# Attention emitted by a table of times per quad of heads, with four score banks and the value product among the transposes' banks

## The chip, the cores and the metric

The kernel runs on one core of a Trainium2 chip. Its engines are PE (matmul), DVE (VectorE), ACT (ScalarE), POOL (GpSimd) and SP (which here only issues DMAs). The metric is device time in microseconds (us), lower is better.

## What is computed

Three stages in a row: windowed attention with a few global tokens, a mixture of experts with one expert per token, and a dense two-layer net.

```
s_g  = scale * q_g @ k_all^T ; out_g = softmax(s_g) @ v_all      # 32 global queries, 544 keys
s_ll = scale * q_l @ k_l^T, masked to |i - j| <= 32              # 512 local queries
s_l  = concat(scale * q_l @ k_g^T, s_ll) ; out_l = softmax(s_l) @ concat(v_g, v_l)
x    = concat(out_g, out_l), 2176 rows (4 batches x 544) of 512 (8 heads x 64)
e    = argmax(x @ w_gate) ; x = gate * relu(x @ w1[e]) @ w2[e]   # 8 experts, one per token
h    = x @ w_in ; g = 0, (h+1)^2/4 or h by pieces ; out = g @ w_out
```

There are 32 heads in all (4 batches of 8). All data is float32; the matmuls of the second and third stage are split into three products of rounded parts, those of the attention are plain float32.

## The kernel before

The change lies in the attention, the first 124 us. The other stages follow it in the program.

**Tiles.** Heads are worked in pairs (`c`, 16 of them) and quads (`q`, 8 of them, two pairs each). The steps, with the letters used below, are:

- G, `s_glob(q)`: scores of a quad's global queries, 12 matmuls into a score bank `sp` and a corner of the bank `gxb`; needs `qg` and the keys of both pairs. GM (`g_max`), GE (`g_exp`), GN (`g_norm`): their maximum on DVE, exponentials on ACT, reciprocal on DVE. TG (`t_glob`): six transposes into two `ps_o` banks, copied out by ACT. PG (`pv_glob`): product with the values of both pairs.
- S, `s_pair(c)`: scores of a pair's two heads, 64 small matmuls and two mask matmuls into two `sp` banks. M (`s_max(n)`): maximum of one head on DVE. E (`s_exp(n)`): four exponentials on ACT. T (`t_head(n)`): four transposes on PE into a `ps_o` bank, copied to `pto` by DVE.
- P, `pv(c)`: product of a pair with its values, 64 matmuls into a bank `xo`, scaled by DVE into `xr`. X (`x_turn`): four transposes of `xr` into a `ps_x` bank, copied by ACT into `xT`. XS (`x_store`): the store of two pairs.
- L and LT (`logits`, `logits_t`), then R (`route`): the gate of one batch, some nine small DVE operations. `early` follows it: a few small matmuls (`ranks`), six to eight DVE operations (`place`) and four POOL operations (`low_hot`). They are put into the list `fill`, of which F (`s_rest`) emits up to eight at a time. `zlist` is a last short chain of matmuls on what `low_hot` wrote. Z runs what stands in `tasks`.
- V and K: loads of values (three DMAs for a pair), keys and queries. V also has POOL spread a pair's values (`spread_v`).

**Banks.** Eight in PSUM: `gxb`, three of tag "s" for scores (S and G), one of tag "x" for `xo`, three of tag "to" for transposes and logits.

**Order.** The program order is the order on each engine: each of PE, DVE, ACT and SP works its instructions strictly as emitted. Before, a loop over 40 steps (`units`, one head or one quad's global part each) emits them: a step first turns the head of two steps ago, then emits its scores, its maxima, the products that are due and its exponentials. The steps of the quads 0, 1 and 7 are moved by hand. After the loop the last two heads, the last two products and the remaining turns are written out. SP's loads are paced: each waits until those more than 1.5 MB ahead of it have landed (`dma`).

Of the kernel before, what the change touches and what calls it, by code (L numbers as in the profile page):

```python
# [8 lines left out]
F32 = mybir.dt.float32  # L9
# [15 lines left out]
B, H, SL, SG, D = 4, 8, 512, 32, 64  # L25
# [5 lines left out]
S = SL + SG  # L31
N = B * S
NT = N // 128
E, F = 8, 1024
# [89 lines left out]
def emit(tc, d, out):  # L124
# [55 lines left out]
    wz = ap.tile([128, 2], F32, name="wz")  # L180
    nc.vector.memset(wz, 0.0)
    nc.scalar.activation(wz[:, 1:2], wz[:, 0:1], AF.Exp)
    wps = ps.tile([128, 512], F32, tag="s", name="sp", bufs=3)
    for _ in range(9):
        nc.tensor.matmul(wps, lhsT=warm[:, 0:128], rhs=warm, start=True, stop=True)
    qp = {}
# [57 lines left out]
    def s_pair(c):  # L244
        k, q = ks[c], qp[c]
        for z in range(2):
            home, n = ("x", 1) if c == 1 and z else ("s", 3)
            sps[2 * c + z] = ps.tile([128, 4, BW], F32, tag=home, name="sp", bufs=n)
        for j in range(NG):
            i, a = divmod(j, 4)  # L250
            for z in range(2):
                r = slice(64 * z, 64 * z + 64)
                nc.tensor.matmul(sps[2 * c + z][a * WIN:(a + 1) * WIN, i, :], lhsT=q[r, j * WIN:(j + 1) * WIN],  # L253
                                 rhs=k_at(k, r, j), start=(i == 0), stop=False)
        for z in range(2):
            nc.tensor.matmul(sps[2 * c + z][:, :, 0:MW], lhsT=mask[:, 0:128], rhs=mask[:, 128:].rearrange("p (i w) -> p i w", i=4), start=False, stop=True)
# [24 lines left out]
        pexp[n] = p  # L281

    def s_glob(q):
        sp = ps.tile([128, 512], F32, tag="s", name="sp", bufs=3)
        for part in range(3):
            for j in range(4):
                c, z = 2 * q + j // 2, 64 * (j % 2)
                k = ks[c][z:z + 64].rearrange("p (n w) -> p n w", w=WIN)
                p = slice(j * SG, (j + 1) * SG)
                o, r = ((sp[p, 0:320], ks[c][z:z + 64, 0:320]),  # L290
                        (sp[p, 320:480], k[:, 15:24:2, :]), (gxb[p, 0:64], k[:, 10:13:2, :]))[part]
                nc.tensor.matmul(o, lhsT=qg[z:z + 64, c, :], rhs=r, start=True, stop=True)
        gsp[q] = sp
# [75 lines left out]
    def pv(c):  # L369
        b, g = divmod(c, 4)  # L370
        p, v = pt.pop(c), vt[c]
        if g == 0:
            xr[b] = ap.tile([128, 4, DM], F32, tag="xr", name="xr", bufs=2)
            xT[b] = ap.tile([128, 4, SL], F32, tag="xT", name="xT", bufs=2)
        xo = ps.tile([128, 4, 2, D], F32, tag="s" if c == 15 else "x", name="xo", bufs=3 if c == 15 else 1)
        for i in range(4):
            for z in range(2):
                for a in range(4):
                    j = 4 * i + a
                    nc.tensor.matmul(xo[a * WIN:(a + 1) * WIN, i, z, :], lhsT=p[:, z, j * WIN:(j + 1) * WIN],  # L380
                                     rhs=v[:, v_at(j), 64 * z:64 * z + 64], start=True, stop=True)
        r = ap.tile([128, 4, 2], F32, tag="ri", name="ri", bufs=3)
        nc.vector.tensor_scalar_add(r, ss[b][:, :, 2 * g:2 * g + 2], 1e-9)
        nc.vector.reciprocal(r, r)
        nc.vector.tensor_tensor(xr[b][:, :, g * 128:(g + 1) * 128].rearrange("p i (z d) -> p i z d", z=2), xo,
                                r.unsqueeze(3).to_broadcast([128, 4, 2, D]), ALU.mult)
# [175 lines left out]
    def zsteps():  # L562
        o = ps.tile([128, 4, 128], F32, tag="to", name="ps_x", bufs=3)
        for k in range(4):
            nc.tensor.transpose(o[:, k, :], xz[:, k * 128:(k + 1) * 128], ident)
        nc.scalar.activation(xzT, o, AF.Copy)
        yield
        for g in range(2):
            o = ps.tile([128, 4, 128], F32, tag="x" if g else "s", name="zh", bufs=1 if g else 3)
            for u in range(4):  # L570
                f = slice((4 * g + u) * 128, (4 * g + u + 1) * 128)
                for k in range(4):
                    nc.tensor.matmul(o[:, u, :], lhsT=w1r[k][:, f], rhs=xzT[:, k, :], start=(k == 0), stop=(k == 3))
                    if u < 3 or k < 3:
                        yield
            nc.scalar.activation(hz[g], o, AF.Relu)
            yield
        o = ps.tile([128, 512], F32, tag="y", name="yp", bufs=2)
        for u in range(4):
            c = slice(u * 128, (u + 1) * 128)  # L580
            for f in range(8):
                nc.tensor.matmul(o[:, c], lhsT=w2r[f // 2][:, f % 2, c], rhs=hz[f // 4][:, f % 4, :], start=(f == 0), stop=(f == 7))
                if (u, f) in ((2, 7), (3, 3)):
                    yield
        yz = mp.tile([128, YW], F32, tag="y", name="y", bufs=3)
        nc.scalar.activation(yz[:, 0:DM], o, AF.Copy)
        for u in range(4):
            nc.sync.dma_start(ys[u][:, 0:128], yz[:, u * 128:(u + 1) * 128])
        put_ids(xz, zpos)
# [4 lines left out]
        for _ in range(n):  # L594
            next(zgen, None)

    units = []
    for q in range(8):
        units += [("g", q), ("h", 4 * q), ("h", 4 * q + 1), ("h", 4 * q + 2), ("h", 4 * q + 3)]
    units.remove(("g", 0))  # L600
    units.insert(3, ("g", 0))
    units.remove(("g", 1))
    units.insert(7, ("g", 1))
    units.remove(("g", 7))
    units.insert(units.index(("h", 27)), ("g", 7))
    raw = [lambda k=k: dma(w1r[k], d["w1"][0, k * 128:(k + 1) * 128, :]) for k in range(4)]
    raw += [lambda k=k: dma(w2r[k], d["w2"][0, k * 256:(k + 1) * 256, :].rearrange("(t p) f -> p t f", p=128))
            for k in range(4)]
# [5 lines left out]
    nc.sync.dma_start(ident, d["ident"])  # L614
    load_k(1)
    load_q(1)
    load_v(0)
    nc.sync.dma_start(qg, d["qg"])
    load_k(2)
    load_q(2)  # L620
    load_v(1)
# [10 lines left out]
    nc.gpsimd.tensor_copy(gid[:, :, 1:2], C("ids").unsqueeze(2))  # L632
    for c in range(3):
        spread_v(c)
    pend_n, pend_g, pend_v = [], [], []
    moved.clear()
    LT, LG = 2, 3
    nv = 3
    for s in range(len(units)):
        kind, a = units[s]  # L640
        tk, ta = units[s - LT] if s >= LT else (None, None)
        if tk == "h":
            t_head(ta)
        gq = units[s - LG] if s >= LG else (None, None)
        if gq[0] == "g":
            t_glob(gq[1])
            pend_g.append(gq[1])
        if kind == "h":
            if a % 2 == 0 and a != 2:
                s_pair(a // 2)  # L650
            if a == 1:
                s_pair(1)
        elif kind == "g":
            s_glob(a)
        while tasks:
            if tasks.pop(0)() == 1:
                break
        if kind == "h" and a % 2 == 1:
            if a // 2 + 4 < 16:
                load_k(a // 2 + 4)  # L660
            if a // 2 + 3 < 16:
                load_q(a // 2 + 3)
        if (kind, a) == ("g", 0):
            s_max(3)
        if kind == "h" and a < 31 and a != 3:
            s_max(a)
        if kind == "h" and a == 30:
            s_max(31)
        elif kind == "g":
            g_max(a)  # L670
        if (kind, a) == ("g", 0):
            s_exp(3)
        for q in pend_g:
            if gq == ("g", q):
                continue
            pv_glob(q)
        for c in pend_v:
            pv(c)
            if nv < 16:
                load_v(nv)  # L680
                nv += 1
            if 0 < c < 14:
                spread_v(c + 2)
            b, g = divmod(c, 4)
            if g % 2:
                tasks.append(lambda b=b, g=g: x_store(b, g // 2))
            tasks.append(lambda b=b, g=g: x_turn(b, g))
            if b < B - 1 and g == 3:
                then = [lambda b=b: tasks.append(lambda: early(b))]
                tasks += [lambda b=b: logits(b), lambda b=b: logits_t(b),  # L690
                          lambda b=b, then=then: fill.extend(route(b) + then)]
        for q in pend_n:
            g_norm(q)
        pend_n, pend_g, pend_v = [], [q for q in pend_g if gq == ("g", q)], []
        if tk == "h" and ta % 2 == 1:
            pend_v.append(ta // 2)
        if kind == "h" and a != 3:
            s_exp(a)
        elif kind == "g":
            g_exp(a)  # L700
            pend_n.append(a)
        if kind == "h":
            s_rest(RATE)
        for _ in range([7, 5, 3, 1].count(len(units) - s)):
            raw.pop(0)()
    assert not fill, len(fill)
    weigh(xz, 128, nc.gpsimd)
    t_head(30)
    pv(14)
    t_head(31)  # L710
    for t in tasks:
        t()
    dma(xs[B * SL:N, 0:DM], xrg)
    glob_turn()
    pv(15)
# [753 lines left out]
```

## Time and profile before

| | |
|---|---|
| median of 3 runs | 740.49 us (738.86 to 744.5) |
| profiled execution | 741.64 us, of which the profile spans 739.8 us |
| PE busy | 711.3 us (96%) |
| DVE, ACT, POOL busy | 486.1 (66%), 332.1 (45%), 150.2 us (20%) |
| mean granted TensorE clock | 0.992 |

How to read it: the first S starts at 4.80 us and the last P ends at 123.38 us; that stretch is the attention. The profiled execution lies 1.15 us above the median. Busy shares over the whole span say little about the attention, since it is one sixth of it.

### The profile page before, as it was taken

How to read it: one execution, taken by the hardware profiler on the slowest of the kernel's cores; microseconds unless marked ns; L12 is line 12 of the kernel's file. 1: busy time of each engine (PE TensorE's matmuls, PEld its weight loads, DVE VectorE, ACT ScalarE, POOL GpSimd, SP SyncE). 2: the span in 40 equal slices, each digit the busy share in tenths (PEclk: the TensorE clock that was granted, in tenths of full speed). 3: DMA queues.
4: the chain of work that ended last, by engine and by line, in shares of the span. 5: the costliest groups of instructions: out<-in, count | busy, mean ns of one | idle time of the engine just before them, and what ended most of it. 6: DMA issues, size and time to landing. Idle time of an engine off the chain costs nothing.

```text
span 739.8 us, 16419 instructions
## 1 busy us (share of the span) xinstructions
PE 711.3 (96%) x6609; PEld 637.6 (86%) x6609; DVE 486.1 (66%) x887; ACT 332.1 (45%) x762; POOL 150.2 (20%) x185
## 2 busy tenths in 40 slices
PE   6889888999999999999999999999999999999995
PEld 4666666999999999899998898999989898998984
DVE  4778885674516478875777678758775876645443
ACT  4757664453525457664564543233323332322220
POOL 3445543677641340000000000000000000011112
PEclk9999999999999999999999999999999999999998
DMA  8786666485658578763531321101110100001111
GB/s 280 237 258 202 203 194 186 134 291 196 190 166 301 199 252 305 244 208 104 122 99 58 105 68 57 58 1 58 57 58 1 58 0 1 1 30 57 43 43 71
DMA packets 52254, 96.07 MB, mean 130 GB/s; under 512 B 9817, under 2 KB 27769, under 8 KB 50128
## 3 DMA queue, kind: packets, MB, share of 16 engines
q1 hardware_dynamic: 48704, 84.75, 36.1%
q0 software_dynamic: 3472, 10.25, 4.2%
q8 instruction: 53, 0.87, 0.5%
q14 instruction: 25, 0.20, 0.1%
HBM read 80.28 MB, written 14.75 MB: 128 GB/s over the span
## 4 chain that ended last, share of the span: by engine, by line
PE 79%; issue 8%; DVE 7%; ACT 2%; DMA 2%; POOL 1%; SPq 0%; POOLq 0%; ACTq 0%; DVEq 0%
PE fh L988 7%; PE fh L986 7%; PE fh L987 7%; PE o L988 6%; PE o L987 6%; PE o L986 6%; PE hp L988 4%; PE hp L986 4%; PE hp L987 4%; PE yp L986 4%; PE yp L987 4%; PE yp L988 4%; PE ps_o L335 2%; PE sp L253 2%; DMA ks<-in_k 2%
## 5 line engine op out<-in xcount | busy, mean ns | idle before, releaser
L1318 DVE SCALAR_TENSOR_TENSOR r<-r 128x384 f32<-128x384 f32 (+1 forms) x96 | 51.4, 535 | 113.4 <-ACT r L1317 113.4
L986 PE MATMUL o<-wh,gh 128*128 128x512 f32 x272 | 106.9, 393 | 0.8 <-ACT acc L1367 0.8
L988 PE MATMUL o<-wh,gl 128*128 128x512 f32 x272 | 107.6, 396 | 0.0
L987 PE MATMUL o<-wl,gh 128*128 128x512 f32 x272 | 107.3, 394 | 0.0
L1371 POOL DMA_INDIRECT out_dram<-acc,rid x17 | 16.5, 969 | 446.4 <-DVE acc L1369 444.8
L1320 ACT ACTIVATE gh<-g 128x384 fp32r<-128x384 f32 (+1 forms) x96 | 48.8, 508 | 129.2 <-DVE g L1319 129.2
L988 PE MATMUL fh<-yh,wl 128*128 128x384 f32 (+1 forms) x320 | 104.3, 326 | 0.0
L986 PE MATMUL fh<-yh,wh 128*128 128x384 f32 (+1 forms) x320 | 104.2, 326 | 0.0
L987 PE MATMUL fh<-yl,wh 128*128 128x384 f32 (+1 forms) x320 | 104.2, 326 | 0.0
L1317 ACT ACTIVATE r<-fh,half 128x384 f32<-128x384 f32 (+1 forms) x96 | 54.0, 562 | 105.6 <-PE fh L988 105.0
L986 PEld LDWEIGHTS fh<-yh,wh 128*128 128x128 f32 x320 | 60.2, 188 | 3.5
L987 PEld LDWEIGHTS fh<-yl,wh 128*128 128x128 f32 x320 | 60.2, 188 | 3.4
L988 PEld LDWEIGHTS o<-wh,gl 128*128 128x128 f32 x272 | 51.1, 188 | 12.4 <-DVE gl L1326 0.4
L988 PEld LDWEIGHTS fh<-yh,wl 128*128 128x128 f32 x320 | 60.2, 188 | 0.0
L986 PEld LDWEIGHTS o<-wh,gh 128*128 128x128 f32 x272 | 51.1, 188 | 9.1 <-ACT acc L1367 1.2
L987 PEld LDWEIGHTS o<-wl,gh 128*128 128x128 f32 x272 | 51.1, 188 | 8.1
L280 ACT ACTIVATE p<-sp,mn 128x128 f32<-128x128 f32 x128 | 45.2, 373 | 20.0 <-DVE mn L263 10.1
L1319 DVE TENSOR_TENSOR g<-r,fh 128x384 f32<-128x384 f32 (+1 forms) x96 | 51.0, 532 | 3.3
L986 PE MATMUL yp<-hTh,w2h 128*128 128x256 f32 (+5 forms) x176 | 51.7, 294 | 0.0
L988 PE MATMUL yp<-hTh,w2l 128*128 128x256 f32 (+5 forms) x176 | 51.2, 291 | 0.0
L987 PE MATMUL yp<-hTl,w2h 128*128 128x256 f32 (+5 forms) x176 | 51.1, 290 | 0.0
L1326 DVE TENSOR_TENSOR gl<-g,gh 128x384 fp32r<-128x384 f32 (+1 forms) x96 | 50.7, 529 | 0.0
(238 smaller groups left out, 1617.3 us busy)
## 6 DMA issues: line engine op xcount, KB each, us to landing
w1r<-in_w SPq DMA_DIRECT2D x32, 512.0 KB
w2r<-in_w SPq DMA_DIRECT2D x32, 512.0 KB
wraw<-in_wf SPq DMA_DIRECT2D x16, 1024.0 KB
ks<-in_k SPq DMA_DIRECT2D x16, 400.0 KB
v<-in_v SPq DMA_DIRECT2D x16, 384.0 KB
yr<-ys SPq DMA_DIRECT2D x68, 64.0 KB
qp<-in_q SPq DMA_DIRECT2D x16, 256.0 KB
xs<-xr SPq DMA_DIRECT2D x8, 512.0 KB
```

The source lines that it names most:

```text
L253: nc.tensor.matmul(sps[2 * c + z][a * WIN:(a + 1) * WIN, i, :], lhsT=q[r, j * WIN:(j + 1) * WIN], rhs=k_at(k, r, j), start=(i == 0), stop= ...
L280: nc.scalar.activation(p[:, i, :].rearrange("p (a b w) -> p a b w", a=2, b=2), v, AF.Exp, bias=mn[:, i:i + 1], scale=scale, accum_out=ss[b ...
L335: nc.tensor.transpose(o[:, i, :], p[:, i, :], ident)
L986: nc.tensor.matmul(o, lhsT=ah, rhs=bh, start=first, stop=False)
L987: nc.tensor.matmul(o, lhsT=ah, rhs=bl, start=False, stop=False)
L988: nc.tensor.matmul(o, lhsT=al, rhs=bh, start=False, stop=last)
L1317: nc.scalar.activation(r[:, 0:w], o[:, 0:w], AF.Relu, bias=half, scale=0.5)
L1318: nc.vector.scalar_tensor_tensor(r[:, 0:w], r[:, 0:w], 1.0, r[:, 0:w], ALU.min, ALU.mult)
L1319: nc.vector.tensor_tensor(g[:, 0:w], r[:, 0:w], o[:, 0:w], ALU.max)
L1320: nc.scalar.activation(gh[:, 0:w], g[:, 0:w], AF.Copy)
L1326: nc.vector.tensor_tensor(gl[:, 0:w], g[:, 0:w], gh[:, 0:w].bitcast(F32), ALU.subtract)
L1371: w = nc.gpsimd.indirect_dma_start(out=out, out_offset=bass.IndirectOffsetOnAxis(ap=rid[:, tt:tt + 1].bitcast(U32), axis=0), in_=a, in_off ...
```

## The change

The loop over `units` is replaced by a table: each step has one or more times in units of a quad (`TIMES`), quad `q` adds `q` to them, `SHIFT` moves the global steps of quads 0 and 1, and all steps are emitted in the order of their times. The banks of tag "x" go to the scores, which have four ("s"); `xo` is put among the three of tag "to". The load of `qg` is issued before the first values. The first four expert weights (`W`) have times of their own.

```diff
-            home, n = ("x", 1) if c == 1 and z else ("s", 3)
-            sps[2 * c + z] = ps.tile([128, 4, BW], F32, tag=home, name="sp", bufs=n)
+            sps[2 * c + z] = ps.tile([128, 4, BW], F32, tag="s", name="sp", bufs=4)
...
-        xo = ps.tile([128, 4, 2, D], F32, tag="s" if c == 15 else "x", name="xo", bufs=3 if c == 15 else 1)
+        xo = ps.tile([128, 4, 2, D], F32, tag="to", name="xo", bufs=3)
...
     load_k(1)
     load_q(1)
+    nc.sync.dma_start(qg, d["qg"])
     load_v(0)
-    nc.sync.dma_start(qg, d["qg"])
...
-    for s in range(len(units)):
-        kind, a = units[s]
...
+    TIMES = {"G": (-0.01,), "GM": (0.051,), "GE": (0.219,), "GN": (0.481,), "TG": (0.505,), "PG": (0.761,), "S": (0.233, 0.574,), ...
+    SHIFT = {("G", 0): -0.168, ("GM", 0): 0.478, ("GE", 0): 0.495, ...
...
+    for t, nm, n in sorted(plan):
+        if (nm, n) not in LAST:
+            JOBS[nm](n)
     t_head(30)
     pv(14)
     t_head(31)
-    for t in tasks:
-        t()
+    s_rest(99)
+    later(0)
+    s_rest(99)
+    later(0)
+    assert not fill and not tasks
+    weigh(xz, 128, nc.gpsimd)
+    x_turn(B - 1, 1)
```

On PE at the start of the program, before: the two pairs' scores come first, and the first quad's global scores (the rows with `qg`) after eight transposes.

```order
L253 MATMUL sp<-ks,qp 32x128 x32
L256 LDWEIGHTS mask
L256 MATMUL sp<-mask 128x4x96
L256 LDWEIGHTS mask
L256 MATMUL sp<-mask 128x4x96
L253 MATMUL sp<-ks,qp 32x128 x32
L256 LDWEIGHTS mask
L256 MATMUL sp<-mask 128x4x96
L256 LDWEIGHTS mask
L256 MATMUL sp<-mask 128x4x96
L335 MATMUL ps_o<-ident,p 128x128 x8
L292 MATMUL sp<-ks,qg 32x320 x4
```

The same place after the change: the global scores are the first work, so PE's first wait is for `qg` and the keys of pair 1.

```order
L291 MATMUL sp<-ks,qg 32x320 x4
L291 MATMUL sp<-ks,qg 32x160 x4
L291 MATMUL gxb<-ks,qg 32x64 x4
L252 MATMUL sp<-ks,qp 32x128 x32
L255 LDWEIGHTS mask
L255 MATMUL sp<-mask 128x4x96
L255 LDWEIGHTS mask
L255 MATMUL sp<-mask 128x4x96
L252 MATMUL sp<-ks,qp 32x128 x32
```

On PE in the middle (from the global scores of quad 5 on; `ps_o` with `p` is T, `xo` is P, `lg` is LT, `ps_x` is X, `ps_o` with `pgz` is TG), before: a T stands between every two larger steps.

```order
L292 MATMUL gxb<-ks,qg 32x64 x4
L411 MATMUL lg<-ident,lgt 128x128 x4
L380 MATMUL xo<-v,pto 32x64 x32
L335 MATMUL ps_o<-ident,p 128x128 x4
L253 MATMUL sp<-ks,qp 32x128 x32
L256 LDWEIGHTS mask
L256 MATMUL sp<-mask 128x4x96
L256 LDWEIGHTS mask
L256 MATMUL sp<-mask 128x4x96
L395 MATMUL ps_x<-ident,xr 128x128 x4
L380 MATMUL xo<-v,pto 32x64 x32
L335 MATMUL ps_o<-ident,p 128x128 x4
```

The same place after: two heads are turned in one go (x8) behind the first P, and the second P follows S and X.

```order
L291 MATMUL gxb<-ks,qg 32x64 x4
L410 MATMUL lg<-ident,lgt 128x128 x4
L379 MATMUL xo<-v,pto 32x64 x32
L334 MATMUL ps_o<-ident,p 128x128 x8
L252 MATMUL sp<-ks,qp 32x128 x32
L255 LDWEIGHTS mask
L255 MATMUL sp<-mask 128x4x96
L255 LDWEIGHTS mask
L255 MATMUL sp<-mask 128x4x96
L394 MATMUL ps_x<-ident,xr 128x128 x4
L379 MATMUL xo<-v,pto 32x64 x32
```

On DVE at the same place, before (`xr` is P's scaling, `pto` the copy of a T, `mx` and `mn` a maximum, `rg` is GN, L457 to L463 are the first operations of a batch's `route`):

```order
L385 TENSOR_TENSOR xr<-xo,ri 128x4x128
L336 COPY pto<-ps_o 128x512
L262 TENSOR_REDUCE mx_1822<-sp 128x4
L263 TENSOR_SCALAR mn<-mx_1822 128x4
L322 TENSOR_SCALAR rg<-sg 128x1
L323 TENSOR_SCALAR rg<-sg,rg 128x1
L324 RECIPROCAL rg<-rg 128x1
L457 TENSOR_REDUCE L<-lg 128x32
L459 TENSOR_REDUCE mx<-L 128x4
L460 TENSOR_TENSOR L<-L,mx 128x32
L461 SCALAR_TENSOR_TENSOR sc<-L,cst 128x32
```

The same place after: the copies of two T stand behind eight operations of the routing.

```order
L384 TENSOR_TENSOR xr<-xo,ri 128x4x128
L456 TENSOR_REDUCE L<-lg 128x32
L458 TENSOR_REDUCE mx<-L 128x4
L459 TENSOR_TENSOR L<-L,mx 128x32
L460 SCALAR_TENSOR_TENSOR sc<-L,cst 128x32
L461 TENSOR_REDUCE m_1749<-sc 128x4
L462 TENSOR_TENSOR oh<-sc,m_1749 128x32
L463 TENSOR_REDUCE se<-ex 128x4
L464 TENSOR_SCALAR se<-se 128x4
L335 COPY pto<-ps_o 128x512 x2
```

The routing has moved ahead of a copy, a maximum and GN: what the next P needs now comes behind it.

## Rows read from the trace of the kernel before

**Rows 1.** The page, part 2: PE's busy tenths in 40 slices of the span

```profile
PE   6889888999999999999999999999999999999995
```

**Rows 2.** Busy us of each engine in stretches: the attention, one quad with routing, one without

```profile
4.80:123.38 118.58, 100.83 (x2957) 74.99 (x2958) 91.13 (x258) 73.72 (x341) 54.71 (x97) 0.97 0.74 224
...
43.08:60.69 17.61, 13.53 (x372) 9.97 (x371) 13.56 (x37) 9.94 (x49) 8.12 (x15) 0.94 0.73 216
60.69:74.28 13.59, 13.52 (x371) 9.65 (x371) 10.88 (x31) 9.16 (x43) 7.51 (x12) 0.95 0.74 229
```

**Rows 3.** PE's waits from 4 to 124 us: us in total, times, longest

```profile
PE ps_x L395 <- DVE pto L336: 4.0, 2, 2.1
...
PE ps_o L335 <- DVE pto L336: 2.0, 2, 1.9
PE sp L253 <- issue: 1.9, 1, 1.9
...
PE xo L380 <- issue: 1.4, 1, 1.4
```

**Rows 4.** Timeline of the start: start us, us, engine, line, operation

```profile
4.80 1.15 PE L253 MATMUL sp<-ks,qp 64*32 64x128 f32 x64 [0.16 <-DMA qp<-in_q]
...
5.30 0.42 SPq L618 DMA_DIRECT2D qg<-in_qg  x1
...
8.63 1.15 PE L253 MATMUL sp<-ks,qp 64*32 64x128 f32 x64 [2.25 <-DMA qp<-in_q]
...
9.92 0.82 POOL L225 COPY v<-v 96x768 f32<-96x768 f32 x1 [7.58 <-DMA v<-in_v]
```

**Rows 5.** Groups by form, 4 to 124 us: count, busy us, mean ns of one, idle before

```profile
L280 ACT ACTIVATE p<-sp,mn 128x128 f32<-128x128 f32 x128 | 45.2, 373 | 20.0 <-DVE mn L263 10.1 <-DVE ri L383 6.2 <-DVE gid L466 1.8
...
L262 DVE TENSOR_REDUCE mx<-sp 128x4 f32<-128x512 f32 x32 | 21.9, 683 | 12.2 <-PE sp L256 12.0
L336 DVE COPY pto<-ps_o 128x512 f32<-128x512 f32 x32 | 21.8, 682 | 4.8 <-PE ps_o L335 4.4
```

**Rows 6.** Timeline of PE in a stretch without long waits

```profile
71.73 1.36 PE L402 MATMUL lg<-xT,wg 128*32 128x512 f32 x8
72.61 1.15 PE L356 MATMUL gxb<-v,pgt 128*32 128x64 f32 x48
...
74.28 1.01 PE L292 MATMUL sp<-ks,qg 64*32 64x320 f32 x16
...
75.34 0.66 PE L411 MATMUL lg<-ident,lgt 128*128 128x128 f32 x4
75.92 1.10 PE L380 MATMUL xo<-v,pto 128*32 128x64 f32 x64
76.95 0.66 PE L335 MATMUL ps_o<-ident,p 128*128 128x128 f32 x4
77.54 1.16 PE L253 MATMUL sp<-ks,qp 64*32 64x128 f32 x64
...
78.96 0.60 PE L395 MATMUL ps_x<-ident,xr 128*128 128x128 f32 x4
...
81.81 0.82 PE L346 MATMUL ps_o<-ident,pgz 128*128 128x128 f32 x6
```

**Rows 7.** Timeline of PE around a wait for DVE and after it

```profile
57.21 0.66 PE L395 MATMUL ps_x<-ident,xr 128*128 128x128 f32 x4 [2.09 <-DVE pto L336]
...
60.69 1.60 PE L292 MATMUL sp<-ks,qg 64*32 64x320 f32 x16
```

**Rows 8.** Timeline of PE: G of quads 2 and 7, and the last P

```profile
30.65 1.01 PE L292 MATMUL sp<-ks,qg 64*32 64x320 f32 x16
...
99.38 1.01 PE L292 MATMUL sp<-ks,qg 64*32 64x320 f32 x16
...
122.39 0.99 PE L380 MATMUL xo<-v,pto 128*32 128x64 f32 x56 [0.88 <-DVE pto L336]
```

**Rows 9.** Timeline of POOL: the last block's `low_hot` before `zlist`

```profile
111.99 3.11 POOL L486 TENSOR_SCALAR ohl<-iota,plf,cst 128x128 f16<-128x128 f16 x4 [1.33 <-DVE plf L504]
```

More of the change, by code (lines that the diff above doesn't have):

```diff
@@ L182, in emit @@
     nc.scalar.activation(wz[:, 1:2], wz[:, 0:1], AF.Exp)
-    wps = ps.tile([128, 512], F32, tag="s", name="sp", bufs=3)
+    wps = ps.tile([128, 512], F32, tag="s", name="sp", bufs=4)
     for _ in range(9):
@@ L283, in s_glob @@
     def s_glob(q):
-        sp = ps.tile([128, 512], F32, tag="s", name="sp", bufs=3)
+        sp = ps.tile([128, 512], F32, tag="s", name="sp", bufs=4)
         for part in range(3):
@@ L568, in zsteps @@
         for g in range(2):
-            o = ps.tile([128, 4, 128], F32, tag="x" if g else "s", name="zh", bufs=1 if g else 3)
+            o = ps.tile([128, 4, 128], F32, tag="s", name="zh", bufs=4)
             for u in range(4):
@@ L595, in zz @@
             next(zgen, None)
[L597 to L605, printed above, removed]
     raw = [lambda k=k: dma(w1r[k], d["w1"][0, k * 128:(k + 1) * 128, :]) for k in range(4)]
@@ L634, in emit, with values, ahead, later @@
         spread_v(c)
-    pend_n, pend_g, pend_v = [], [], []
     moved.clear()
-    LT, LG = 2, 3
-    nv = 3
-    for s in range(len(units)):
-        kind, a = units[s]
[L641 to L654, printed above, removed]
+    def values(c):
+        if c + 3 < 16:
+            load_v(c + 3)
+        if 0 < c < 14:
+            spread_v(c + 2)
+    def ahead(c):
+        if c + 4 < 16:
+            load_k(c + 4)
+        if c + 3 < 16:
+            load_q(c + 3)
+    def later(_):
         while tasks:
@@ L657, in emit @@
                 break
[L658 to L706, printed above, removed]
@@ L707, in emit, with routed, work, weight @@
-    weigh(xz, 128, nc.gpsimd)
+    def routed(b):
+        fill.extend(route(b) + [lambda: tasks.append(lambda: early(b))])
+    def work(_):
+        s_rest(RATE)
+    def weight(k):
+        raw.pop(0)()
+    JOBS = {"G": s_glob, "GM": g_max, "GE": g_exp, "GN": g_norm, "TG": t_glob, "PG": pv_glob, "S": s_pair, "M": s_max, "E": s_exp,
+            "T": t_head, "P": pv, "V": values, "X": lambda c: x_turn(*divmod(c, 4)), "XS": lambda h: x_store(*divmod(h, 2)), "K": ahead,
+            "F": work, "Z": later, "L": logits, "LT": logits_t, "R": routed, "W": weight}
@@ new lines, in emit @@
+    TIMES = {"G": (-0.01,), "GM": (0.051,), "GE": (0.219,), "GN": (0.481,), "TG": (0.505,), "PG": (0.761,), "S": (0.233, 0.574,), "M": (0.259, 0.387, 0.683, 0.797,), "E": (0.358, 0.636, 0.817, 1.058,), "T": (0.755, 0.861, 1.216, 1.219,), "P": (1.099, 1.472,), "V": (1.191, 1.63,), "X": (1.278, 1.7,), "XS": (1.991,), "K": (0.685, 1.489,), "F": (0.252, 0.681, 0.177, 0.898,), "Z": (0.598, 0.159, 0.495, 0.715, 1.027,), "L": (2.825,), "LT": (3.094,), "R": (3.103,)}
+    SHIFT = {("G", 0): -0.168, ("GM", 0): 0.478, ("GE", 0): 0.495, ("GN", 0): 0.518, ("G", 1): -0.116, ("GM", 1): 0.159, ("GE", 1): 0.248, ("GN", 1): 0.125, ("TG", 0): 0.542, ("PG", 0): 0.628, ("TG", 1): 0.779, ("PG", 1): 0.639}
@@ new lines, in emit @@
+    WEIGHTS = (7.629, 6.164, 8.624, 7.969)
+    LAST = {("T", 30), ("T", 31), ("P", 14), ("P", 15), ("X", 13), ("X", 14), ("X", 15), ("XS", 7)}
+    plan = []
+    for nm, when in TIMES.items():
+        per = len(when)
+        for n in range(per * 8 if nm not in ("L", "LT", "R") else B - 1):
+            q, k = divmod(n, per) if nm not in ("L", "LT", "R") else (2 * n, 0)
+            plan.append((q + when[k] + SHIFT.get((nm, n), 0.0), nm, n))
+    plan += [(t, "W", n) for n, t in enumerate(WEIGHTS)]
```

## The prediction

> **What bounds the kernel now.** First the page's slices: PE is at nine tenths or more from the seventh slice to the last but one, and below in most of the first six, the attention [rows 1]. So the stages behind it are PE's own work and will only be moved; what is to be won or lost lies in the first 123.38 us. Then the busy time of that stretch: of 118.58 us PE is busy 100.83, DVE 91.13 and ACT 73.72 [rows 2]. No engine is full; PE and DVE wait for each other in turn. PE's busy time also holds waits (a transpose that stands open for its exponentials counts), so PE's own work is less, and DVE's 91 us are nearly as near to being the bound. The waits name the exchange: PE waited 4.0 and 2.0 us for DVE's copies `pto`, and 1.9 and 1.4 us as "issue", for nothing that the profile shows [rows 3]. The question is then how long a quad takes, how late it starts, and what the end costs.
>
> **What does not change.** The table emits the same matmuls, copies and exponentials; their own cost is nil. The program behind the last P is emitted as before: the second half of the first expert's weights is still loaded behind the last store, and the fourth of the first half now leaves SP at the first store before the end, with three T and two P (nearly 4 us, at the prices below) and the last gate ahead of its first use. If that cover were gone, PE would wait there for part of one 512 KB load. So a gain or a loss at the last P goes through to the end.
>
> **The start.** Before, PE had its first scores at 4.80 us, when the queries of pair 0 landed, and the next at 8.63, when those of pair 1 did [rows 4]. Now G of quad 0 is first on PE, and S of pairs 0 and 1 are queued behind it, with all of DVE and ACT behind those. It needs `qg`, which SP issues now between the queries of pair 1 (landed by 8.63) and the first values (POOL got them at 9.92) [rows 4]. The landing lies between 8.63 and 9.92; by its 256 KB against the 384 KB of the first value load behind it I take 9.4. PE is then idle for 4.8 us after its warm-up.
>
> What that idle time does to the clock is open in this trace. After a wait of 2.09 us a G took 1.60 us in place of 1.01 [rows 7, 6], at a granted clock of 0.94 to 0.95 over those quads [rows 2]; after a wait of 2.25 us an S kept its 1.15 [rows 4]. The new gap is longer than both, so I take the slow price for G and, as an estimate by the same ratio on a part of it, for the first S: 1.8 and 1.9 us with their small rows, 1.2 more than at full clock. The Trainium skill, "TensorE: Matmul & The Clock Gate", "HAM oscillation — how this bites in real kernels", says that long idle gaps of PE bring its clock down to half, so that the next work starts cold; the 1.60 us agrees, the 1.15 us does not. By the rule the start is as I sum it, by the 1.15 us it is 1.2 us earlier.
>
> So G ends at 11.2, S of pair 0 at 13.1, S of pair 1 at 14.6. From there ACT is the chain: a head's four exponentials are 4 x 0.373 = 1.5, overlapped to about 1.4 [rows 5]; before the third G come six heads (8.4), two global exps of three activations each (2 x 1.3, an estimate from three such rows that are longer), the copies of a TG (0.9) and of an X (0.6), 12.5 in all, from 14.0 on. In between ACT waits some 2.2 us: S of pair 2 stands on PE behind T of head 3, which waits for that head's exponentials, and its maximum comes 2 us later. T of head 5 closes at 29.0, and G of quad 2 begins at 29.0. Before, it began at 30.65 [rows 8]. The late start would so be won back before the third quad, though in part because less has been done by then: the new order owes one T, one TG and one P more at this point, which the next two sums hold.
>
> **A quad.** PE's own work, from start to start [rows 6]: G 1.06, P 1.03, T 0.59, S 1.42; from durations X 0.60, TG 0.82, PG 1.15. One G, TG, PG, two P, S, X and four T: 11.5, less some 0.3 by which durations overlap the next start, 11.2. Following the new order through one quad, with each maximum at 0.68 + 0.17 and each copy at 0.68 [rows 5], nothing on PE waits: G and P pass while the fourth head's exponentials run, the two T come just after them, S and X cover the two copies (1.4 us) that the second P needs, and the next maxima fall into TG and S. The bank of `xo` is free when its third successor needs it, since two T, an S and an X lie between. DVE's quad without routing is 10.88 [rows 2], within 11.2. ACT's 9.16 is too.
>
> Quads 2 to 6 are then: quad 2, with TG and PG of quad 1 moved into it and an L (0.88 [rows 6]), 11.2 + 0.8 + 1.1 + 0.9 = 14.0. Quads 3 and 5 with routing: DVE had 13.56 there [rows 2], PE 12.0 with LT (0.58) and `ranks`; since the copies stand behind eight operations of the routing now, PE's second P waits, and I take DVE's time and 0.4 for the exchange, 14.0 each. Quads 4 and 6, with an L, 12.1 each. Sum 66.2, against 68.73 from G of quad 2 to G of quad 7 before [rows 8], where PG of quad 6 and the last L had not been done yet.
>
> **The end.** From G of quad 7: one G, LT, TG, PG, four P, six T, two S, three turns, `ranks` and the list, 16.3. Two waits are added by the table: P of pair 13 behind the routing on DVE, 1.5; and `zlist`, which now comes some 4 us after `ranks`, while the maxima and copies on DVE and POOL's four `low_hot` (3.11 us [rows 9]) lie between, 2.3. Queued behind it are the last two T and P. Sum 20.1, against 24.0 before (99.38 to 123.38 [rows 8]).
>
> **"Issue".** The two waits of 1.93 and 1.41 us [rows 3] belong to no wait of the order. They may come again (3.3) or not (0); where DVE is behind they cost nothing. I take 1.5.
>
> **Sum.** 29.0 + 66.2 + 20.1 + 1.5 = 116.8 for the end of the last P, 6.6 before the 123.38 of before. From the profiled 741.64 that is 735.0; from the median, which lies 1.15 lower, 733.9.
>
> **The rivals.**
> *DVE stays full.* DVE's 91.13 us in the attention hold its waits for POOL too; if the first maximum comes at 13.0 and DVE then idles only 4 to 8 us, the last P ends at 108 to 112, 11 to 15 us early: 726 to 730. For it: in my start DVE has little idle time, and my quads leave it 0.3 to 1. Against it: the routing quads and the end, where it waits for PE in my sum.
>
> *The shared ring.* `xo` now takes a bank in turn with T, X and TG. A P whose scaling waits on DVE (behind a maximum or the routing) holds a third of the banks of all transposes, PE's next T, X or TG is queued behind that on PE, and the next maxima behind those. If that costs 0.8 us in each of eight quads, the gain is gone: 740.5. For it: PE's longest waits were on DVE's copies out of this ring [rows 3]. Against it: two S and two X of a quad lie where the bank is needed. It is also the case in which the table doesn't do what it says.
>
> *The late start stays.* The first scores come 4.6 us later and 1.2 slower, and V of pair 0, the loads of the third values, now goes ahead of the keys of pair 5 in SP's queue, where it waits for PG of quad 0. If G of quad 2 waits for those keys and starts 5.8 us later than before (36.4), and the quads take what they took (68.73 / 5 = 13.7), the time is 746.3, slower. It decides if the mean quad stays over 12.5 (13.7 less 5.8 / 5). For it: the loads of the start made PE wait for 2.25 us already [rows 4]. Against it: PG of quad 0 ends near 25 in my walk, and if the 1.29 us from 8.63 to 9.92 [rows 4] brought the 384 KB of a value load, the 960 KB up to those keys take 3.2 us, to 28.2.
>
> **How the numbers follow.** The forecast, with its unknowns (landing 8.6 to 9.9, the clock 1.2, "issue" 0 to 3.3, the routing waits doubled or gone), spans a gain of 3 to 10 and has a chance of 0.54; DVE stays full 0.18; the shared ring 0.20; the late start 0.08. Less than 1% (7.4 us, about what this measurement can tell from no change) is most of the forecast and all of the ring. Faster by over 1%: 0.18 and 0.45 of the forecast, 0.42. Slower by over 1%: 0.05 of the late start, whose 5.8 us lies inside 1% unless more is added. Within: 0.53. The range leaves out the lower half of DVE's case and the late start: 728.5 to 741.0.
>
> **What would show it.** In the trace after: the first G on PE between 8.6 and 10 us, with 1.4 to 1.7 us for its wide matmuls; G of quad 2 at 28 to 30; quads of 12 to 14 us; PE's waits on `pto` only in routing quads; a wait of about 2 us before `zlist`; the last P at 114 to 120. It is wrong if G of quad 2 comes after 32, if quads without routing take over 13, or if PE waits for `xr` or `pto` in each quad.

## The result and the profile after

| | before | after |
|---|---|---|
| median (range), runs | 742.51 us (736.27 to 746.87), 20 | 749.24 us (742.12 to 756.47), 20 |
| ratio of after to before, 95% interval | | 1.0058 [1.0031, 1.0086] |
| the same again, on another chip | 740.37 us (738.22 to 743.84), 23 | 743.96 us (739.19 to 748.66), 10; 1.0053 [1.0025, 1.0081] |

The changed kernel is slower by 0.6%, where 733.9 us was forecast. The ratios here and below leave out executions that were disturbed, the medians do not.

Its runs lie over a range of 14 us, and the profiled execution, 756.37 us with a span of 754.5, is near the top of that range. So the unedited kernel was profiled once more (run a0_same: 739.19 us, span 737.3, the shortest of its thirty runs). Both are read here.

> The changed kernel unedited, for a second profile and as the mark for the other three. The first profile of it lay at the slow end (756.4 us, against 742 to 756 in twenty runs). Theory A (the start): G first, half clock until about 22 us, and the keys of pair 5 held behind values that wait for PG of quad 0: G of quad 2 done after 34 us here again, in a fast run as in a slow one. Theory B (PE's 'issue' holes): the sum of PE's waits named issue from 4 to 130 us is 4 us or more above that of before (3.3) and moves with the run's time. Theory C (the shared ring of transposes): PE waits for xr, pto or xT in every quad. Time 742 to 756.

PE's waits from 4 to 135 us in the profile after, which answer to [rows 3] (us in total, times, longest):

```profile
PE sp L252 <- issue: 4.1, 4, 1.6
PE sp L291 <- DMA qg<-in_qg: 3.9, 1, 3.9
PE xo L379 <- issue: 2.2, 2, 1.9
PE sp L291 <- DMA ks<-in_k: 2.0, 1, 2.0
PE sp L252 <- ACT p L279: 1.7, 1, 1.7
...
PE ip L535 <- DVE zc L520: 1.5, 1, 1.5
PE gxb L355 <- issue: 1.4, 1, 1.4
...
PE xo L379 <- DVE pto L335: 0.9, 1, 0.9
```

The waits for `pto` are down from 6.9 us to 0.9. Before, the 4.0 and 2.0 us of [rows 3] and this line:

```profile
PE xo L380 <- DVE pto L336: 0.9, 1, 0.9
```

All waits for DVE together fall less, from 8.1 to 5.2 us, since other copies and maxima take their place. "Issue" is 7.7 us in seven waits, against 3.3 in two. The timeline of PE in the same profile, which answers to [rows 4, 8] (the first G, G of quads 2 and 7, the last P):

```profile
8.80 1.82 PE L291 MATMUL sp<-ks,qg 64*32 64x320 f32 x16 [3.88 <-DMA qg<-in_qg]
...
34.66 0.79 PE L291 MATMUL sp<-ks,qg 64*32 64x320 f32 x8 [1.97 <-DMA ks<-in_k]
...
108.64 1.01 PE L291 MATMUL sp<-ks,qg 64*32 64x320 f32 x16
...
131.18 1.10 PE L379 MATMUL xo<-v,pto 128*32 128x64 f32 x64
```

The last P ends at 132.28, 8.9 us later than before. From there to the end it is 622.2 us, against 616.4 before and 616.2 in a0_same; 2.4 of the 5.8 us are waits called "issue" again (at 181 to 184 us, in the second stage), the rest was not followed.

PE's waits in a0_same, and the same places of its timeline:

```profile
PE sp L252 <- issue: 3.4, 7, 0.8
...
PE ip L535 <- DVE och L513: 2.7, 1, 2.7
PE sp L252 <- ACT p L279: 2.0, 2, 1.7
PE xo L379 <- DVE mg L303: 1.6, 1, 1.6
PE ps_o L334 <- DVE xr L384: 1.1, 3, 0.5
PE xo L379 <- DVE pto L335: 0.6, 1, 0.6
PE xo L379 <- issue: 0.6, 1, 0.6
PE ps_o L334 <- issue: 0.6, 1, 0.6
```

```profile
8.40 1.83 PE L291 MATMUL sp<-ks,qg 64*32 64x320 f32 x16 [3.18 <-DMA qg<-in_qg]
...
30.21 0.73 PE L291 MATMUL sp<-ks,qg 64*32 64x320 f32 x4
...
100.45 1.01 PE L291 MATMUL sp<-ks,qg 64*32 64x320 f32 x16
...
120.02 1.10 PE L379 MATMUL xo<-v,pto 128*32 128x64 f32 x64
```

Here "issue" is 4.6 us in nine waits, and the waits for DVE are 6.0 in all. The last P ends at 121.12, 2.3 us earlier than before, where 6.6 were forecast.

### The profile page after: what moved, and what is told of

Its sections match the earlier page's. It is cut to its first block, busy times and chain, and to the rows that moved or that the text cites. A ratio compares the mean times of both kernels' runs of the same rounds, so it can differ in the third digit from the quotient of the medians.

```text
span 754.5 us, 16402 instructions
## 1 busy us (share of the span) xinstructions
PE 717.8 (95%) x6609; PEld 642.3 (85%) x6609; DVE 482.6 (64%) x887; ACT 331.4 (44%) x762; POOL 150.3 (20%) x185
## 3 DMA queue, kind: packets, MB, share of 16 engines
q0 software_dynamic: 3472, 10.25, 4.1%
## 4 chain that ended last, share of the span: by engine, by line
PE 62%; issue 7%; DVE 4%; ACT 2%; POOL 1%; DMA 1%; another core or an unknown queue 1%; POOLq 0%; SPq 0%; ACTq 0%; DVEq 0%
PE fh L955 7%; PE fh L953 7%; PE fh L954 7%; PE o L955 6%; PE o L954 6%; PE o L953 6%; PE hp L955 4%; PE hp L953 4%; PE hp L954 4%; PE yp L953 4%; PE yp L955 3%; PE yp L954 3%; POOL out_dram L1338 1%; PE xTp L908 1%
```

## The experiments

All times below are medians; "1.0053" and the like are ratios to the kernel before, run beside it.

### The start

My first theory was the late start: keys that come late (`ks`, 1.97 us above), a clock that falls while PE waits (the granted clock was 0.50 from 10 to 20 us in the profile after), and the first scores behind `qg`. The rival was that the start is won back later, whatever it costs.

e1_keys loads the keys ahead of the values:

```diff
-"K": (0.685, 1.489,)
+"K": (0.685, 1.185,)
```

> The second keys and queries of a quad go ahead of its first values in SP's order (K's second time 1.489 to 1.185). Theory A: keys of pair 5 no longer wait for PG of quad 0, the wait of 2 us on DMA ks in G of quad 2 is gone, G of quad 2 done by 32, 2 to 4 us faster than the unedited kernel. Theory B: no change in the sum of issue waits, since the same bytes are moved, so within 1 us. Theory C: no change.

743.87 us, 1.0053 [1.0022, 1.0083]: as without the edit. The wait for `ks` is gone, the time is not.

e2_g0late puts G of quad 0 behind the first two pairs' scores, as before the change:

```diff
-SHIFT = {("G", 0): -0.168, ("GM", 0): 0.478,
+SHIFT = {("G", 0): 0.61, ("GM", 0): 0.633,
```

> G of quad 0 and its maximum moved behind the scores of the first two pairs, as before the change; the load of qg stays where the change put it. Theory A: first scores at 4.8 us again, full clock from there, 3 to 5 us faster than the unedited kernel, if the late start and its half clock are what is paid. If the exponentials of the first heads and the loads set the pace up to quad 2, under 1.5 us. Theories B and C: no change.

746.65 us, 1.0098 [1.0064, 1.0132]. The first S started at 4.98 again, but the second only at 9.42, behind its queries, and G of quads 1 and 2 then waited 6.5 us for keys. So the loads set this start, not the place of the first G.

e3_warm keeps PE busy until `qg` lands:

```diff
-    for _ in range(9):
+    for _ in range(20):
         nc.tensor.matmul(wps, lhsT=warm[:, 0:128], rhs=warm, start=True, stop=True)
```

> Eleven more warm-up matmuls (9 to 20), which keep PE busy until about 9 us; nothing else changes. If the half clock of the start is what costs, G takes 1.0 in place of 1.8 us, S 1.2 in place of 2.0, and the kernel is 2 to 4 us faster than unedited. If PE goes back to half clock anyway because it waits between its first steps, or if ACT and DMA set the pace there, within 1 us.

745.52 us, 1.0074 [1.0041, 1.0107]. The first G takes 1.01 us in place of 1.82, so its price was right; but waits for keys (2.3 us) and "issue" (6.6 us) take it back.

e8_fifth (with the edit of e1_keys) gives pair 1 a fifth score bank, since its S had waited 1.7 us for the first head's exponentials (`S <- ACT p` above):

```diff
+            home, n = ("to", 3) if c == 1 and z else ("s", 4)
...
-("TG", 0): 0.542
+("TG", 0): 0.575
```

> The changed kernel with the keys ahead and the second bank of pair 1's scores taken from the transposes' banks, so that S of pair 1 need not wait for the first head's exponentials; TG of quad 0 moves behind the fourth head's exponentials. If that wait (1.7 to 2.1 us) is what made the start late: G of quad 2 at 28.5 to 30, and 741 to 743 us. If ACT is the chain there anyway, as my sum of the start had it, G of quad 2 stays at 31 and the time at 743 to 745.

743.35 us, 1.0030 [1.0003, 1.0058]. That wait is gone; but G of quad 2 starts at 32.63, later than either figure expected, behind 1.7 us for POOL's values and 1.3 of "issue". No single wait of the start is worth its length.

### The banks

e4_xbank gives the new order the banks of before (three of tag "s", `xo` alone in "x"); b1_banks gives the order before the new banks. The diff is that of e4_xbank:

```diff
-tag="s", name="sp", bufs=4
+tag="s", name="sp", bufs=3
...
-        xo = ps.tile([128, 4, 2, D], F32, tag="to", name="xo", bufs=3)
+        xo = ps.tile([128, 4, 2, D], F32, tag="x", name="xo", bufs=1)
```

> The table with the banks of before: three score banks, and a bank of its own for the value product. Theory C (shared ring): waits for xr before transposes (three of 0.3 to 0.5 us in the unedited kernel) vanish, 2 to 6 us faster than unedited. Theory D: the ring is not what is paid; the missing score bank makes S wait for exponentials instead, 0 to 5 us slower than unedited.

752.06 us, 1.0133 [1.0073, 1.0193]: S waited 5.2 us in eight places for exponentials that still held a bank.

> The kernel before with only the banks changed (four score banks, xo among the transposes' three), order and loads as before. My rival of the shared ring: every T, X and TG can stand behind a P whose scaling waits, so 743 to 747. Otherwise, if the bank split alone is worth what the run with the table and the old banks suggests (8 us there), 734 to 738. The old order never has three pairs' scores open, so I expect little: 739 to 742.

745.76 us, 1.0078 [1.0049, 1.0107]. Its longest group of waits is that of my rival, the shared ring:

```profile
PE ps_o L345 <- DVE xr L384: 7.2, 5, 2.9
```

TG waits for a bank that P's scaling still holds. The ring costs about what the rival said (7.2 us of waits, 4.8 us in the median), but in the old order; in the new one T waits for P's scaling 1.1 us in three places. The new order is slower with the old banks, and the old order with the new ones.

### The pacing of the loads

e6_room lets 1.0 MB be in flight in place of 1.5; r1_room6 (with the edit of e1_keys) and r2_before_room6 (the kernel before) let 3 MB, `ROOM = 6.0`.

```diff
-    ROOM = 3.0
+    ROOM = 2.0
```

> The pacing of SP's loads at 1.0 MB in place of 1.5 MB. Theory B (PE's instructions are fetched behind the bulk loads): with fewer bytes in flight each hole shortens by a third, so the sum of issue waits falls from about 5 to 3 us, 1 to 3 us faster than unedited. Theory D (keys and values late): loads start later, waits on DMA ks grow, 1 to 5 us slower. Both at once: within 1 us.

755.75 us, 1.0193 [1.0137, 1.0249], with 10.1 us of "issue" (4.6 in a0_same) and 4.2 of waiting for values.

> The changed kernel with the keys ahead (K at 1.185, as in the run with that edit alone, 743.87 us) and the pacing of SP's loads widened from 1.5 to 3 MB in flight. Theory A (loads come late: the tighter pacing of 1.0 MB cost 11.9 us in waits for values and in issue holes): wider pacing gives part of it back, last P at 117 to 119, 738 to 741 us, PE's waits for DMA gone. Theory B (the holes come from how many bytes stand in the DMA queues ahead of PE's instructions): more in flight makes the holes longer, 748 or more. No difference (743 to 745) if the buffers of keys, queries and values, not the pacing, hold the loads back.

747.12 us, 1.0074 [1.0043, 1.0105]. "Issue" is 6.4 us (5.6 in e1_keys) in a profiled execution of 738.16 us, the shortest that was profiled here.

> The kernel before with the pacing widened from 1.5 to 3 MB. Theory A: same or up to 2 us faster (its waits for loads were small). Theory B: slower, 743 to 747, with more than the 3.3 us of issue holes that it had. If the old order is as indifferent as I think, 740 to 742.

741.76 us, 1.0017 [0.9991, 1.0043], "issue" 3.8 against 3.3. Less in flight goes with more "issue", and more in flight changes it by under 1 us: by these single profiles the waits don't grow with the bytes that the pacing lets be in flight.

### The loads away

n1_after_noload and n2_before_noload leave out the loads of keys from pair 4 and of queries and values from pair 3 on, and use the data of earlier pairs; n3_after_novalues leaves out only the values. The outputs are others and the experts' part differs, so only the attention is read. The edit of the values (keys and queries get the like in n1 and n2):

```diff
     def load_v(c):
+        if c > 2:
+            vt[c] = vt[c - 3]
+            return
```

> The changed kernel without the loads of keys of pairs 4 to 15 and of queries and values of pairs 3 to 15; those pairs work on the data of pairs 0 to 3, so the attention is computed for repeated data and the experts get other tokens. Only the attention is read (end of the last P). Theory D (loads): what the clean order needs is the last P at 113 to 117 us (my sum without the 1.5 us of issue, less what key loads cost), PE's issue waits fall under 1.5 us in all, and no wait on DMA after 20 us. Theory B' (issue holes are PE's own fetch, whatever DMA does): holes stay at 3 us or more. Theory C (ring): the last P stays at 119 or later, with waits for pto, xr or xT in each quad.

> The kernel before without the same loads, as the partner of the run above; again the later pairs work on repeated data. Theory D: the old order is bound by its own exchange of PE, DVE and ACT, so it gains little, last P at 119 to 122 us against 123.4, and the new order's advantage without loads is 4 to 7 us. If the old order gains as much as the new one, loads do not explain why the table gave no gain.

> The changed kernel without the loads of the values of pairs 3 to 15 (560 of some 1216 KB for each pair); the data of earlier pairs are used again, so the output is another. Only the attention is read. Theory F: the requests for instructions are put back less, holes between the 0.8 us of the run without any loads and the 5 to 8 us of the runs with all of them, 2 to 4 us; last P at 118 to 121 with a clock that stays up. Rival (the loads' own landing is what costs): holes as before, 4 us or more, and the gain, if any, in waits for DMA.

From G of quad 2 to G of quad 7 the new order takes 66.39 us without loads, the old one 65.61, with 3,813 and 3,553 instructions on PE; the last P ends at 121.6 and 120.1. "Issue" is 0.8 us in n1, but the waits for `pto` come back (0.6 in a0_same):

```profile
PE xo L388 <- DVE pto L344: 3.7, 9, 0.8
...
PE sp L261 <- issue: 0.8, 2, 0.5
```

In n2 "issue" is 3.6 us, 3.0 of it in one wait at 109 to 112 us, where the first expert's weights are loaded. With half of the loads (n3) it is 4.7 us, more than I gave it, and the quads take 71.11. Each is one execution, and n1's first G came at 10.25, 1.85 us later than in a0_same; from G of quad 2 to the end of the last P n1 takes 88.9 us and n2 90.5, their "issue" included. So the 4 to 7 us that I expected of the new order without loads do not show. "Issue" is less where the loads of the attention are gone, but half of the loads gave as much of it as all of them in a0_same.

### Where the waits called issue stand

Many of them come back at the same matmuls of the same steps from run to run. PE in a0_same, and in e3_warm, whose 11 more warm-up matmuls are 22 more instructions with their weight loads:

```profile
41.38 0.84 PE L252 MATMUL sp<-ks,qp 64*32 64x128 f32 x35 [0.58 <-issue]
...
51.31 0.45 PE L252 MATMUL sp<-ks,qp 64*32 64x128 f32 x15 [0.46 <-issue]
```

```profile
43.31 0.92 PE L252 MATMUL sp<-ks,qp 64*32 64x128 f32 x46 [0.21 <-issue]
...
53.84 0.65 PE L252 MATMUL sp<-ks,qp 64*32 64x128 f32 x26 [0.55 <-issue]
```

35 and 15 matmuls of an S were still to come; now 46 and 26, eleven more. Counted over the records of PE, 14 of the 16 such waits in the attention of a0_same and after are at a multiple of 256 instructions plus one constant, and so are both of the kernel before, the 1.93 and 1.41 us of [rows 3]. The trace also has a queue of instruction packets of 16 KB, 53 in the whole program. Each of the 14 waits ends 1.2 to 1.6 us after such a packet has ended, and those two 1.6 and 1.2 us after. So PE stands still because its next 256 instructions aren't there (theory F in the texts of the runs). In those 14 the packet had started 0.6 to 4.0 us after PE entered the block (256 instructions) before, which so lasted 3.4 to 6.6 us; what sets when it starts is not shown. u1_small measures that by itself, ahead of the attention:

```diff
+    for n in range(2048):
+        g = slice(32 * (n % 4), 32 * (n % 4) + 32)
+        nc.tensor.matmul(wps[g, 0:32], lhsT=warm[g, 0:32], rhs=warm[g, 0:32], start=True, stop=True)
```

> The changed kernel with 2048 matmuls of 32 columns in front of the attention, four at a time in the four quarters of the array (2048 weight loads and 2048 matmuls, 16 blocks of 256 instructions); they use no data, and run while the first loads (some 5 MB) land and on after that. All else is the same, and only this stretch is read. Theory F (PE's instructions come in blocks of 256, 16 KB each, one at a time: a block is asked for after PE has entered the one before, takes about 1 us and can be used some 1.3 us after that, and loads put the request back): with nothing else to wait for PE stops at the same count modulo 256 in every block, a block lasts 3.0 to 3.5 us once the loads are done, and 4 us or more while they run. Rival (the holes are made by the attention's own steps): the 16 blocks run without holes, each in the time of its matmuls, 2.3 to 3.4 us by the S of 64 matmuls in 1.15 us, and loads make no difference.

PE's timeline, five of the blocks (x128 are 128 matmuls, with as many weight loads 256 instructions):

```profile
11.55 1.22 PE L188 MATMUL sp<-warm 32*32 32x32 bf16 x128 [4.48 <-issue]
16.65 1.22 PE L188 MATMUL sp<-warm 32*32 32x32 bf16 x128 [3.88 <-issue]
21.20 1.22 PE L188 MATMUL sp<-warm 32*32 32x32 bf16 x128 [3.33 <-issue]
...
28.38 1.22 PE L188 MATMUL sp<-warm 32*32 32x32 bf16 x128 [2.24 <-issue]
...
62.21 1.22 PE L188 MATMUL sp<-warm 32*32 32x32 bf16 x128 [2.51 <-issue]
```

A block comes 5.10 and 4.55 us after the one before while the first loads run (DMA busy 0.80 from 10 to 20 us), and 3.76 on the mean of the nine from 28.38 to 62.21, somewhat more than the 3.0 to 3.5 expected. From 30 to 50 us the view of DMA shows only the instructions, five packets:

```profile
DMA packets 5, 0.08 MB, mean 4 GB/s; under 512 B 0, under 2 KB 0, under 8 KB 0
...
q8 instruction: 5, 0.08, 1.6%
```

By the packets' records a block's packet starts 1.1 to 1.7 us after PE entered the block before it, 2.5 and 2.0 beside loads; it takes 0.9 to 1.5 us, and PE goes on 1.3 to 1.6 us after its end.

### Instructions that cost PE little

Three kernels get 1024 instructions more, 64 ahead of each pair's scores: the changed one (x1), the one before (x2), and n1 (x3, with its other output).

```diff
     def s_pair(c):
...
+        for n in range(32):
+            g = slice(32 * (n % 4), 32 * (n % 4) + 32)
+            nc.tensor.matmul(sps[2 * c][g, 0, 0:32], lhsT=warm[g, 0:32], rhs=warm[g, 0:32], start=True, stop=True)
```

> The changed kernel with 32 matmuls of 32 columns (64 instructions) put ahead of the scores of each pair, 1024 instructions in the attention; they use no data and are overwritten. In the run with such matmuls alone 256 instructions took PE 1.22 us at half clock when they were there, so that these 1024 cost PE 2.4 to 4.9 us, while 256 of them came no faster than every 4.6 to 5.1 us beside loads and 3.7 without. Theory F (with loads PE works at the rate at which its instructions come): 4 blocks more at 4.6 to 5.1 us, 18 to 20 us where no slack is left, 10 to 20 in all: 754 to 764 us, with the waits called issue up by as much. Rival (PE's own time and the exchange with DVE and ACT): 2 to 5 us, 746 to 749.

> The same 1024 instructions in the kernel before. Theory F: 23 blocks in 118 us are 5.1 us each, so it stands near the same rate: 8 to 18 us more, 749 to 759. Rival: 2 to 5 us, 743 to 746.

> The same 1024 instructions in the changed kernel without the loads of keys, queries and values behind the first buffers (the output is another; only the attention is read; last P at 121.6 without the 1024). Theory F: 743 + 128 instructions a quad are 3.4 blocks, at 3.7 us 12.6 us, against some 13.3 us that the quads take for other reasons: 2 to 6 us more, last P at 124 to 128. Rival: the same 2 to 5 us as with loads.

x1: 762.18 us, 1.0299 [1.0267, 1.0332]. x2: 752.03 us, 1.0143 [1.0110, 1.0176]. So 18.2 us more than a0_same's median and 10.8 more than the kernel before, for 4.8 us of PE's time (in x1's timeline 32 of the matmuls, where they don't wait, take 0.30 us from start to start). PE's waits called issue in x1:

```profile
PE sp L255 <- issue: 7.0, 4, 2.2
...
PE xo L382 <- issue: 3.3, 4, 1.4
PE sp L250 <- issue: 2.4, 1, 2.4
PE gxb L358 <- issue: 2.3, 2, 1.8
...
PE sp L258 <- issue: 0.5, 1, 0.5
```

They are 15.5 us, against 4.6 in a0_same, and 11.0 in x2, against 3.3 before. x3's last P ends at 132.35, 10.7 us later than n1's: both theories gave less. "Issue" is 9.7 us there against 0.8, so the supply holds PE up without loads too, once there are more instructions; 2.9 of it is one wait near the end, beside the load of the first expert's weights.

The stretches from G of quad 2 to G of quad 7 (us; then the busy us of PE with the matmuls, of the weight loads with their number, and of the other engines; last the granted clock, the DMA share and GB/s), before, in a0_same and in x1:

```profile
30.65:99.38 68.73, 62.21 (x1777) 45.65 (x1776) 56.18 (x153) 44.71 (x204) 33.57 (x59) 0.98 0.74 226
```

```profile
30.21:100.45 70.24, 63.01 (x1908) 46.63 (x1907) 56.20 (x163) 48.86 (x225) 34.21 (x60) 1.00 0.77 239
```

```profile
36.77:119.02 82.25, 70.22 (x2228) 52.77 (x2227) 57.10 (x162) 48.28 (x220) 36.17 (x64) 0.93 0.68 206
```

| G of quad 2 to G of quad 7 | us | instructions | us for 256 |
|---|---|---|---|
| before | 68.73 | 3553 | 4.95 |
| a0_same | 70.24 | 3815 | 4.71 |
| x1, new order and 640 more | 82.25 | 4455 | 4.73 |
| x2, old order and 640 more | 72.56 | 4193 | 4.43 |
| n1, new order, no loads | 66.39 | 3813 | 4.46 |
| n2, old order, no loads | 65.61 | 3553 | 4.73 |
| x3, new order, no loads and 640 more | 72.43 | 4454 | 4.16 |

a0_same and x1 have the same time for 256 instructions, so here more instructions cost their full share of it. It is no floor: x2 took 4.43 us beside the same loads, and in a0_same seven of the 15 blocks have a wait called issue. The old order takes 640 more for 3.8 us there: its waits for `pto` (6.9 us before, 1.5 in x2) had left room. Most of what x2 loses lies ahead of this stretch, where G of quad 2 comes 7.1 us later than before.

### A version without the wait ahead of the list

v1_zlate is e8_fifth with `zlist` behind the last T, so that the 2.7 us in a0_same ahead of it no longer hold two T and two P:

```diff
-    LAST = {("T", 30), ... ("XS", 7)}
+    LAST = {("T", 30), ... ("XS", 7), ("Z", 39)}
```

> A try at a better version: the changed kernel with the keys ahead, the fifth score bank for pair 1, and the list of the last expert (zlist) emitted behind the last T in place of ahead of it; PE waited 2.4 to 2.8 us ahead of zlist in most runs of the changed kernel, with two T and two P queued behind it. If that wait is on the path: 740.5 to 741.5 us, as before or a little under. If the copies of the last T on DVE are what comes last there anyway: 742.5 to 744. Theory F says that neither gets far under the kernel before as long as the loads run beside PE.

748.50 us, 1.0043 [1.0005, 1.0082], above what either case gave. The wait is gone, and in the profiled execution (753.42 us) "issue" is 11.4 us in all, 3.2 of it in one wait near the end (118.41). No version here beats the kernel before.

## Why the prediction was wrong

**"Issue" is the step that failed.** I read the 1.93 and 1.41 us as belonging to no wait of the order and put 1.5 into the sum. They are PE's instructions coming late, and there are more of them in the denser order: 4.6 us in a0_same, 7.7 in the profile after. The whole attention is 5,915 instructions, 23.1 blocks (2,957 matmuls and 2,958 weight loads [rows 2]); at the 4.55 to 5.10 us that two blocks of u1 show beside loads that is, as an estimate, 105 to 118 us, and the attention before took 118.58 in all. Such a limit isn't in my sum, nor among the rivals. It is no strict bound, since x2 took 4.43 us a block. That the supply holds the new order up is shown by x1, with 10.9 us more of "issue" than a0_same. That loads lengthen a block, from 3.76 us to 4.55 and 5.10, is shown by u1; n1 against a0_same agrees (0.8 us against 4.6). How much traffic it takes is open: half of the loads left 4.7 us, and the pacing changed it in no plain way.

**A quad.** 66.2 us were walked for G of quad 2 to G of quad 7; a0_same took 70.24. PE waited 7.1 us there: 3.4 are "issue", and 1.6 are a P of quad 4 behind GM on DVE (`mg`), which the walk did not have. The errors are of both signs. Quads 4 and 6, without routing, took 15.28 and 13.90 (12.1 forecast, and over 13 was named as the sign of being wrong), quad 2 15.49 (14.0); the routing quads 3 and 5 took 13.05 and 12.52 (14.0 each). Without loads (n1) the stretch is 66.39, but this agreement is in part luck: the quads there are 14.98, 12.86, 12.64, 13.53 and 12.38, and PE waited for `pto` in nine places. And I set a walk in which PE hardly waits against 68.73 that was measured with loads and waits; the old order without loads takes 65.61, though with 260 instructions fewer in this stretch. Set like against like, the table shows no clear gain.

**The start.** G came at 8.40 to 8.80 (9.4 forecast) and took the 1.8 us forecast. G of quad 2 came at 30.21 and 31.96, half of it at 34.66, not 29.0: S of pair 1 needs a fifth bank, which I had missed (1.7 us), and the keys of pair 5 came late, as the rival of the late start said, by 0.3 and 1.97 us. Neither is worth its length (e8, e1).

**The end.** 20.67 us in a0_same, 20.1 forecast; the wait ahead of `zlist` 2.7, forecast 2.3. The 1.5 us for P of pair 13 did not come; in its place the P behind the list took 1.94 us for 1.10, at a granted clock of 0.83 from 110 to 120 us, so the sum agrees in part by luck. In the profile after it is 23.64, with 3.6 of "issue" in it.

**The sum.** That of a0_same, 30.21 + 70.24 + 20.67 = 121.12, misses the forecast by 1.2 + 4.0 + 0.6, less the 1.5 that I had put in for "issue": 4.3 us, of which 3.1 are "issue" beyond those 1.5. But a0_same lies 4.8 us under its own median, and that part is not explained run by run. In the profile after the last P comes 11.2 us later than in a0_same: 3.1 more of "issue", 2.4 more of waiting for `qg` and keys, 1.5 for ACT's `xT`, and work at a lower granted clock (0.92 over the attention, 0.99 in a0_same). "Issue" alone does not order the runs: the 738.16 us of r1 had 6.4, the 746.77 of e2 3.7.

**The rivals and a reading.** DVE full: no, its busy time in the attention is 87 us of 116 to 128. The shared ring: true of the banks (b1), not of the new order with them. In [rows 1] PE is at nine tenths from the eighth slice on, not the seventh; nothing hangs on it.

## What to carry to other kernels

Count the instructions that each engine must be fed, not only their time: a stretch of many small matmuls (here 743 instructions in a quad of 13.6 us [rows 2]) can be held up by the supply of instructions, and then filling waits by a denser order gains little. A wait named "issue" that stands at the same count of instructions in every run is the sign; more instructions whose own time on the engine is small and known are the test. And set a walked schedule against a walked one, or a measured against a measured: waits that a walk leaves out are not a gain.

## What was not expected of the hardware

PE took 256 small instructions in 1.22 us and then stood for 2.24 us or more, with no load beside it (u1). The Trainium skill, "Runtime: NRT & Kernel Launch", "Instruction fetch mechanics", says that the instructions come in blocks of 16 KiB (256) and that the cost of crossing from one to the next is mostly hidden. The blocks agree with the 16 KB packets and the count here; the cost does not: 3.76 us a block without loads, for 1.22 us of work, and up to 5.10 with them.

After a wait of 3.88 us G took 1.82 us, after one of 0.71 us (e3) 1.01. In u1, where PE stood idle for two thirds of each block, the granted clock was 0.50 from 10 to 70 us, the lower of its two levels.
